# Attention and a Mish FFN on one core: the order table written anew, and ScalarE's table loads as steps of their own

## The chip, the core and the metric

The kernel runs on one core of a Trainium2 chip. A core has five engines that run side by side, each with its own queue of instructions: TensorE (PE in the profile), VectorE (DVE), ScalarE (ACT), GpSimd (POOL) and SyncE (SP, which here issues the transfers). They wait for each other through semaphores. The metric is device time in microseconds (us), lower is better.

## The reference

Attention over 4 batches x 8 heads x 768 positions x 64, with a mask by hash buckets of 6 bits, and then a feed-forward layer with the Mish function on 3072 tokens:

```python
q_bits = (einsum('bhsd,dk->bhsk', q, proj) > 0)        # k_bits in the same way
mask = q_bucket[:, :, :, None] == k_bucket[:, :, None, :]
scores = where(mask, scale * q @ k.T, -1e9)
attn = exp(scores - max(scores)); attn = attn / (sum(attn) + 1e-9)
x = (attn @ v).transpose(0, 2, 1, 3).reshape(3072, 512)
h = x @ w_in                                            # 512 x 2048
out = (h * tanh(softplus(h))) @ w_out                   # 2048 x 512
```

## The kernel before

The 3072 tokens are cut into 12 units of 256 tokens, three to a batch. A unit has 8 attention slots (4 pairs of heads x 2 halves of the unit's tokens), so there are 96 slots, n = 0 to 95, and 8 feed-forward groups of 256 hidden columns, so 96 groups, m = 0 to 95. A backbone (line 213) lists the large steps of TensorE:

- S n: scores of a slot, 8 matmuls at L878 into the banks ps_s. Behind it VectorE takes the maximum of each row (L884, "max"), derives scale and bias from it (L890, L894, L896, "scl"), and ScalarE takes the exponential twice, one head each (L909, "exp"), which frees ps_s for S n+1.
- After that the probabilities are divided and split into two halves of 16 bits: "hi" (L372, L374 or L375) and "lo" (L390, or L396 and L397), and turned by transfers (L407).
- V p: a pair of slots times the values (L992); "x_hi" and "x_lo" (L1016, L1019) write the unit's input of the feed-forward layer.
- H m: first product of a group (L1048 to L1050), then "mish" on ScalarE (L1066), "g_hi" and "g_lo" (L374 or L375, L390), then O m0 and O m1, the second product for the two halves of the tokens (L1099 to L1101).

Unit 0 is computed in 32-bit floats (S0 to S7, H0 to H7, O00 to O71, the last two at L1044 and L1095), since the weights come as 64-bit numbers that have to be made into 32-bit words first: "w_u" (L372 to L375), "w_sign" (L543, L548), "w_low" (L552, L556, L559) and "w_join" (L563) for each of 16 pieces. After a group's O the pieces are split into 16-bit halves (square L424, a small matmul L457 "st", L461, L446, "w_hi", "w_lo"), and H8, the first group of unit 1, needs the scales of all 16. Inputs of a batch are split likewise ("q_hi", "q_cp", "q_lo", "k_hi", "k_cp", "k_lo", "v_hi", "v_lo", L372 to L397).

Nothing is ordered by a scheduler when the kernel is built. Every step is recorded with its alternatives (engine and a cost in ns), and the table ORDER (L87 to L200) says in which order all 2753 steps are emitted and, by a letter b, c or d behind the number, which alternative is taken, which often means which engine. Each engine runs its own steps in that order. So ORDER decides both the order on each engine and how the work is shared out. ScalarE needs a table of functions for the exponential and another one for Mish; the compiler puts a load ahead of an activation whose table is not there. `port(...)` marks the VectorE alternatives that the search behind the table takes to share a port with GpSimd.

Of the kernel before, what the change touches and what calls it, by code (L numbers as in the profile page):

```python
# [92 lines left out]
71 205b 164 165 464 185 125c 186 188 189 190 174b 126 143b 211 212 206b 207 216b 122 187 200 201 176 167 177 178 180
202 166 191 192 197 198 308 309 372 378 193b 373 374 179 208 458 459 460 194 182d 183 199 225 203 379 128 380 184 127
204 226 248 375 227 222 223 249b 250c 251 254 230b 161 231 376c 229 228 310b 224 240 241 242 232c 233 243 244 245 311b
247 195 268 269 270 246 219c 305 271 209 265 272 196b 210 273 217 253 274b 266 255 461b 236d 237 238 262d 263 465 181
283 284 234 220 275 286 276 267 279c 285 259b 287 221 239 466 235 260 370 293c 292 294 295b 264 252 299 280 281 277
288 289 291 261 290 313c 300 301b 278 326b 462b 296 297 218b 282b 314 306 315 371 321 322 323c 324 312 327 328b 317
325 298 318 316c 432 434 329 330 344d 302 303 352 467 433 456 319 320 345 353 354 304 332b 333 435 347c 346 348 349
463 483 350 351 355 457 484 356 391 334c 335 336 337 468b 357 383b 384 385 441 485 486 392 393 338c 394 387 487 488  # L100
386 443 331 442 339 340c 341 343 503 388 396c 377b 397 381 389 398c 399 489b 444 541 395 469b 491 424 425 436 426c 400
497 527 490 402b 403b 404b 437 438 439 428 440 554 448d 405 504 505 342 406b 470 390 449 450c 452 506 401 445 492 555
580 411b 429 382 471 472 453 412 579 427b 430 493 431 407b 408b 409 410 494 495c 413b 414 358 359 507b 556 473 496
360b 474 498 475c 415 476 477c 479 451 508b 509 564 416c 480 510 454 455 499 500b 417b 557 420 361b 363 418 419 421
422c 423 542 502 516 364 517 518 501 446 565 519b 520 521c 523 362 522 566 543 478b 544 545 528 481 598 600 511 512
513b 514 567 529 530 532 365 558 546c 547 623 515 581 548 622 636 366 368 599 367 582 583 584 525 531 666 533b 534 549
550 447 524 601 602 642 585 586 482 603 536 539 369 551b 552b 553 535 537 526 559 624 625 626 587 588 627b 628b 540
589 590b 560 561 604b 629 591b 592 562 563 571c 568 538 572 574c 667 605 607 655 656 569 674 657 577b 593 594 643 644
645 646 595c 630 631 632 608 573 698 633 575 576 634c 675 647b 648 635 606b 609 610 596 597 637 614b 615 701 702 703
649 704 650 578 705c 651 570 723 616 652b 653b 706 676 677 654 707 638 639 640 713 618 641 619 708 709 715 716 724 719  # L110
720 678 717 617c 669 620 621 718 612 679 680b 658c 710 699 721b 681b 750 611 613 711c 712 700 722 659 661 714 660b 670
671b 732 683 684 746 751 860 747 748 662 663 749 672 664 754 682c 673 727 690c 691 693b 692 752b 757b 725c 726 694 728
767 798 800 733 755 729 730 665 856 731 769 695 696 697 753 807 759b 760 762 758 775 761 768 765 766 763b 764 774 770
771 808 809 810c 734 735 736 820 737c 772 773 801 790b 739 791 857 858 802 685 686 799 806 756 688 861 792 873 687 740
741 859 794 689 795 793 796 811 827 877 803c 804 805 864 821 812 813 814c 816 817 742 855 874 738c 744 862b 743 776
863 822 823b 777 778 779 878 780 781c 783 815b 818 745 875 876 825 894 909 879 880 824 847b 848 850 797 782c 895 910
784 868 869 870 871 849b 851 853 911 945 785 872 886c 887 881 882 896 826 883 786 931 828 829 884b 788 787 865 897
898b 899 830 831 842 819 888b 890b 832 833c 961 835 900 901c 902 852 889b 892b 854 932 933 789 934 912 903 668 913 914
834 964 946 962 905 843 844 845 1147 915 968 916 937b 948 891 965 966b 885 935b 938 904c 907 977 967 997 996 893 906
949 950 969 970c 971 1012 939 941 836 978 979b 951 940c 952 1011 953 908 954 955 867 837 917 846 918 980 838 840 839  # L120
942 1148 947 981 972 943 944 956 959 866 1019 973 974b 841 982 1050 957 958 975 960 919 920 921 976 922c 924 925 988c
989 990c 1102 992 1051 1052b 1046 998 999 1000 991 1047 985 993 994 995 1048c 983b 984 1001 1053 1149 1020 1021 1022
1049 1002 1003c 1004 1005c 1007 1060 1014 1015 1016b 1006 1045 1080 1008 926 927 1009 1010 923c 1064 929 928 930 1018
1017 1023b 1024 1025c 1027 1028 1032 1033 1034 1013 1031 1079 986 987 1061 1026 1029 1030 1062b 1063 1065 1094 1036
1066c 1067 1035 1037c 1038 1040 1273 1068 1039c 1041 1043 1069 1044 1055 1056 1096 1042 1095 1116 1054 1128 1057 1059
1058 1081 1070 936 1071c 1072 1074 1073c 1075 1076 1103 963 1082 1083 1117 1118 1119 1144 1085 1077 1078 1084 1086c
1087 1088 1090 1145b 1150 1146 1151 1152c 1097 1153 1339 1154 1183 1098 1099 1129 1182 1089 1155 1156b 1157 1101 1100
1104 1105 1106 1107c 1108 1091 1163 1164 1092 1131 1120b 1121 1122c 1123 1198 1132 1133b 1167 1109 1134 1124 1135 1232
1233 1168 1169b 1126 1136 1137 1093 1138c 1165c 1166 1158 1159 1110 1160 1161 1197 1140 1162 1111 1112 1113 1125 1139c
1272 1234c 1236 1237 1238b 1170 1141 1246 1247 1174 1184 1250 1235 1251 1142 1171 1185 1186 1187 1127 1130 1175 1176c  # L130
1178 1188 1114 1143 1206 1177c 1180 1179 1181 1189 1190 1207 1192 1191c 1193 1172 1194 1200 1201 1304 1202 1239 1203
1173 1205 1231 1208 1199 1240 1217 1204 1248b 1195 1209b 1210 1212 1252c 1253 1218 1219 1220 1266 1297 1211 1213 1221
# [1122 lines left out]
```

## Time and profile before

| | |
|---|---|
| median of 3 runs | 840.0 us (839.82 to 841.43) |
| profiled execution, its own time | 841.4 us |
| its span from first to last instruction | 839.6 us |
| TensorE busy | 794.9 us, 95% |
| VectorE busy | 714.6 us, 85% |
| ScalarE busy | 632.1 us, 75% |
| GpSimd busy | 93.6 us, 11% |
| granted clock of TensorE | 0.992 of full speed |

Busy times are unions of the engine's records, so a busy TensorE need not be at its peak. Times from the span's start are given as "at 172.3 us". Durations of an instruction are the means of its group.

### The profile page before, as it was taken

To read this page: it belongs to the slowest core of one execution; us is meant where nothing else is said; L and a number is where in the kernel's file an instruction comes from. 1 tells how busy PE (TensorE), PEld (TensorE's weight loads), DVE (VectorE), ACT (ScalarE), POOL (GpSimd) and SP (SyncE) were. 2 spreads that over 40 slices of the span, in tenths; PEclk is the share of its full clock that TensorE was granted. 3 is DMA by queue.
4 is the path that set the end of the run, shared out by engine and by line. 5 is a ranking of instruction groups with operands and counts; after the bars stand their busy time and mean duration, and the time that the engine had idled before them with its cause. 6 is when DMAs were issued, how large, how long until landed. Compare 5 with 4: busy or idle time off the path is not lost. (4 is left out here: it accounts for less than half of the span.)

```text
span 839.6 us, 16631 instructions
## 1 busy us (share of the span) xinstructions
PE 794.9 (95%) x6508; PEld 546.2 (65%) x6508; DVE 714.6 (85%) x1334; ACT 632.1 (75%) x972; POOL 93.6 (11%) x96
## 2 busy tenths in 40 slices
PE   4788989789999999999999999999999999999997
PEld 4656556466668578578577586577577577576664
DVE  6798999898989888989998998899999889888522
ACT  6777889987798687689878688679888688587410
POOL 5445424322230000000000000000000000000000
PEclk9899999999999999999999999999999999999999
DMA  9985878769999869899989987899997848655700
GB/s 281 197 253 178 215 179 195 120 147 186 203 181 181 165 120 158 175 171 180 185 170 175 159 176 154 142 171 196 201 157 159 168 96 160 123 95 102 157 1 26
DMA packets 400303, 135.58 MB, mean 161 GB/s; under 512 B 370528, under 2 KB 391008, under 8 KB 400224
## 3 DMA queue, kind: packets, MB, share of 16 engines
q1 hardware_dynamic: 400224, 134.52, 80.3%
q8 instruction: 51, 0.84, 0.4%
q14 instruction: 28, 0.23, 0.1%
HBM read 35.65 MB, written 6.29 MB: 50 GB/s over the span
## 5 line engine op out<-in xcount | busy, mean ns | idle before, releaser
L909 ACT ACTIVATE pb<-ps_s,svb 128x768 f32<-128x768 f32 x192 | 188.7, 986 | 58.6 <-DVE svb L896 50.6
L1048 PE MATMUL ps_acc<-X,wi 128*128 128x256 f16 x704 | 191.9, 273 | 0.8 <-ACT ffb L1066 0.8
L1050 PE MATMUL ps_acc<-X,wi 128*128 128x256 f16 x704 | 191.8, 273 | 0.0
L1049 PE MATMUL ps_acc<-X,wi 128*128 128x256 f16 x704 | 191.8, 272 | 0.0
L884 DVE TENSOR_REDUCE svb<-ps_s 128x2 f32<-128x1536 f32 x96 | 168.2, 1752 | 14.7 <-PE ps_s L878 11.1
L390 DVE SCALAR_TENSOR_TENSOR hl<-pb,svb,hl 128x768 f16<-128x768 f32 x172 | 174.5, 1022 | 6.5 <-ACT hl L374 4.0
L878 PE MATMUL ps_s<-KT,QT 128*128 128x512 f16 (+1 forms) x768 | 141.8, 328 | 6.3 <-ACT pb L909 5.3
L1099 PE MATMUL ps_o<-wo,ffb 128*128 128x512 f16 x352 | 133.4, 379 | 0.0
L1101 PE MATMUL ps_o<-wo,ffb 128*128 128x512 f16 x352 | 133.4, 379 | 0.0
L1100 PE MATMUL ps_o<-wo,ffb 128*128 128x512 f16 x352 | 133.4, 379 | 0.0
L878 PEld LDWEIGHTS <-QT 128*128 128x128 f16 x768 | 73.3, 98 | 56.6 <-issue 14.5
L374 ACT ACTIVATE hl<-pb,svb 128x768 f16<-128x768 f32 x80 | 73.4, 930 | 35.0 <-DMA PT<-hl 21.4
L992 PE MATMUL ps_t<-PT,VT 128*64 128x256 f16 x1584 | 94.6, 274 | 3.0 <-DMA PT<-hl 2.3
L1066 ACT ACTIVATE ffb<-ps_acc,smalls 128x512 f32<-128x512 f32 x88 | 59.3, 684 | 48.0 <-PE ps_acc L1050 46.9
L992 PEld LDWEIGHTS <-VT 128*64 128x64 f16 x1584 | 83.8, 110 | 17.3 <-issue 16.8
L1049 PEld LDWEIGHTS <-wi 128*128 128x128 f16 x704 | 68.8, 98 | 12.9 <-issue 1.8
L1048 PEld LDWEIGHTS <-wi 128*128 128x128 f16 x704 | 68.8, 98 | 11.6 <-issue 1.6
L1050 PEld LDWEIGHTS <-wi 128*128 128x128 f16 x704 | 68.8, 98 | 8.3 <-issue 0.2
L390 DVE SCALAR_TENSOR_TENSOR ffb<-ffb,smalls 128x512 f16<-128x512 f32 x88 | 65.2, 747 | 3.4 <-ACT ffb L374 0.9
L909 ACT ACT_TABLE_LOAD x45 | 57.7, 1283 | 12.1 <-DVE svb L896 4.7
L1101 PEld LDWEIGHTS <-ffb 128*128 128x128 f16 x352 | 34.4, 98 | 41.5
L1066 ACT ACT_TABLE_LOAD x46 | 59.0, 1283 | 0.8
(212 smaller groups left out, 991.9 us busy)
## 6 DMA issues: line engine op xcount, KB each, us to landing
out_dram<-ffb SPq DMA_DIRECT2D x24, 256.0 KB, 2.8
stg<-in_q_dram SPq DMA_DIRECT2D x10, 512.0 KB, 4.8
stg<-in_k_dram SPq DMA_DIRECT2D x12, 384.0 KB, 3.9
stg<-in_v_dram SPq DMA_DIRECT2D x12, 384.0 KB, 3.6
wo<-in_moe_w_out_dram SPq DMA_DIRECT2D x7, 512.0 KB, 4.9
stg<-in_moe_w_out_dram SPq DMA_DIRECT2D x7, 512.0 KB, 4.4
stg<-in_moe_w_in_dram SPq DMA_DIRECT2D x6, 512.0 KB, 4.5
wi<-in_moe_w_in_dram SPq DMA_DIRECT2D x6, 512.0 KB, 4.5
```

The source lines that it names most:

```text
L390: return [("DVE", 215 + 1.035 * n, port(lambda: nc.vector.scalar_tensor_tensor(out=dst, in0=src, scalar=sc, in1=hi, op0=ALU.mult, op1=ALU. ...
L878: nc.tensor.matmul(sc[:, hh * S + c0 * P:hh * S + c1 * P], QTb[:, u % 2, sl, qi], KTb[:, j, sl, hh * NCH + c0:hh * NCH + c1].rearrange("p ...
L884: op("max", [("DVE", 1790, lambda: nc.vector.tensor_reduce(out=sv[:, 0], in_=sc.rearrange("p (h e) -> p h e", h=2), axis=AX.X, op=ALU.max, ...
L909: EXP[n, hh] = op("exp", [("ACT", 1075, lambda hh=hh, t=t: nc.scalar.activation(pb[:, t], sc[:, hh * S:(hh + 1) * S], AF.Exp, bias=sv[:, 2 ...
L992: nc.tensor.matmul(pv[hh * D:(hh + 1) * D, 0:256], vt[:, w, hh * NCH + c], pt[:, hh, a * NCH + c].rearrange("p s t -> p (s t)"), start=(x ...
L1048: nc.tensor.matmul(o, wh, X[:, 0, c], start=(c == 0), stop=False)
L1049: nc.tensor.matmul(o, wh, X[:, 1, c], start=False, stop=False)
L1050: nc.tensor.matmul(o, wl, X[:, 0, c], start=False, stop=(c == NCC - 1))
L1066: op("mish", [("ACT", 690, lambda: nc.scalar.activation(ffb[:, t], PS[psn], AF.Mish, scale=h))], [psn] + ([(hsn, g, g + 1)] if u else []), ...
L1099: nc.tensor.matmul(PS[f"o{s}"], gh, hi[:, e], start=first, stop=False)
L1100: nc.tensor.matmul(PS[f"o{s}"], gh, lo[:, e], start=False, stop=False)
L1101: nc.tensor.matmul(PS[f"o{s}"], gl, hi[:, e], start=False, stop=last)
```

## The change

Two new steps are recorded. Ahead of the two exponentials of each slot stands "pre_e", ahead of each Mish "pre_m". Each has two alternatives: a load of the table as an instruction of its own, or nothing. They have no predecessors and no readers, so they can stand anywhere in the order. The numbers of all later steps move on, and the table is a new one throughout, 2945 steps; of it the diff shows the first line.

```diff
 ORDER = """
-37 88 14 22 7 0 3 1 2 23 24 25 63 73 38c 6 8 9 13 10 15 152 5 4 40 41 18 19 42 74 11b 12 20 21 26c 53b 75 76 77b 43 28
...
+1 155 0 3 14 22 2 23 24 25 38c 4 40 7 6 8 9 5 10 41 11 12 13 37 18 19 63 73 20 21 26c 42 43 74 44 75 490b 76 39 28b 15
...
     def att_exp(n):
         sv, x = svb[:, n % NSV], f"sv{n % NSV}"
         sc, scn = scores(n)
+        op("pre_e", [("ACT", 1290, lambda: nc.scalar.preload_act_table(AF.Exp)), ("ACT", 0, lambda: None)])
         for hh in range(2):
...
         h = hs[:, g:g + 1] if u else 1.0
+        op("pre_m", [("ACT", 1290, lambda: nc.scalar.preload_act_table(AF.Mish)), ("ACT", 0, lambda: None)])
         op("mish", [("ACT", 690, lambda: nc.scalar.activation(ffb[:, t], PS[psn], AF.Mish, scale=h))],
```

The steps themselves and their data are the same. In the new table 43 pre_e and 22 pre_m are loads, the others nothing; where a table is then still missing the compiler loads it as before, 15 times ahead of an exponential and 32 times ahead of a Mish. With the first load of the program that makes 113 loads where there were 92. The sharing of the work among the engines changes too. On GpSimd, w_sign goes from 8 to 10, v_hi from 2 to 4, w_low from 3 to 4; hi goes from 8 to 5, lo from 4 to 2, v_lo from 2 to none, sums from 6 to 2, k_cp from 4 to 1, g_hi from 4 to none. The lines of the new program lie 9 (up to pre_e), 10 and 11 (behind pre_m) further down.

ScalarE around the Mish of H5 in unit 0 (L909 exp, L1066 mish; in the new program L919 and L1077, the explicit loads L916 and L1076). Before:

```order
L1066 ACT_TABLE_LOAD
L1066 ACTIVATE ffb<-ps_acc_820 128x512
L374 ACTIVATE tok_64<-X,smalls 128x16x64
L424 ACTIVATE wi,smalls<-wi 128x1024
L909 ACT_TABLE_LOAD
L909 ACTIVATE pb,svb<-ps_s,svb 128x768
L1016 ACTIVATE X<-ps_t,smalls 128x256
```

Now:

```order
L1076 ACT_TABLE_LOAD
L1026 ACTIVATE X<-ps_t,smalls 128x256 x2
L1077 ACTIVATE ffb<-ps_acc_824 128x512
L916 ACT_TABLE_LOAD
L433 ACTIVATE wo,smalls<-wo 128x1024
L433 ACTIVATE wi,smalls<-wi 128x1024
L919 ACTIVATE pb,svb<-ps_s,svb 128x768 x2
```

The load of Mish's table now stands two activations ahead of the Mish, and that of the exponential two squares ahead of it.

GpSimd, the end of its queue (L372 hi and g_hi, L396 and L397 the two instructions of a lo, L381 w_home). Before:

```order
L381 TENSOR_SCALAR wo<-stg 128x1024
L372 TENSOR_SCALAR hl<-pb,svb 128x768
L372 TENSOR_SCALAR ffb<-ffb,smalls 128x512
L372 TENSOR_SCALAR hl<-pb,svb 128x768
L396 TENSOR_SCALAR pb<-pb,svb 128x768
L397 TENSOR_TENSOR hl<-pb,hl 128x768
L372 TENSOR_SCALAR ffb<-ffb,smalls 128x512
L890 TENSOR_SCALAR svb<-svb,smalls 128x2
L896 TENSOR_TENSOR svb<-svb 128x2
L372 TENSOR_SCALAR hl<-pb,svb 128x768
```

Now, up to the last instruction:

```order
L406 TENSOR_TENSOR hl<-pb,hl 128x768
L455 TENSOR_SCALAR smalls<-smalls 128x2
L455 TENSOR_SCALAR smalls<-hw 128x1
L381 TENSOR_SCALAR tok_64<-stg,smalls 128x12x64
L390 TENSOR_SCALAR tok_65<-tok_64 128x12x64
L405 TENSOR_SCALAR pb<-pb,svb 128x768
L406 TENSOR_TENSOR hl<-pb,hl 128x768
```

The new queue of GpSimd ends with steps of S16 and S17 and of the inputs of batch 1. What it did later, of slots 18 to 24, is with VectorE and ScalarE now.

VectorE between the max of S29 and that of S30 (L375 hi, L390 lo and g_lo; now L384 and L399). Before:

```order
L390 SCALAR_TENSOR_TENSOR hl<-pb,svb,hl 128x768
L375 TENSOR_SCALAR ffb<-ffb,smalls 128x512
L390 SCALAR_TENSOR_TENSOR ffb<-ffb,smalls 128x512 x2
L642 TENSOR_SCALAR smalls<-ho,smalls 128x8
L446 TENSOR_SCALAR smalls<-smalls 128x8
L1019 SCALAR_TENSOR_TENSOR X<-ps_t,smalls,X 128x256
L390 SCALAR_TENSOR_TENSOR ffb<-ffb,smalls 128x512
L931 RECIPROCAL svb<-svb 128x2
L375 TENSOR_SCALAR hl<-pb,svb 128x768
L390 SCALAR_TENSOR_TENSOR hl<-pb,svb,hl 128x768
```

Now:

```order
L384 TENSOR_SCALAR hl<-pb,svb 128x768
L399 SCALAR_TENSOR_TENSOR hl<-pb,svb,hl 128x768 x2
L784 TENSOR_SCALAR smalls<-smalls 128x4
L455 TENSOR_SCALAR smalls<-smalls 128x4
L399 SCALAR_TENSOR_TENSOR ffb<-ffb,smalls 128x512
L935 TENSOR_SCALAR svb<-svb 128x1 x2
L941 RECIPROCAL svb<-svb 128x2
L384 TENSOR_SCALAR hl<-pb,svb 128x768
L859 TENSOR_SCALAR smalls<-smalls 128x4
L399 SCALAR_TENSOR_TENSOR hl<-pb,svb,hl 128x768
```

Between the two stand one hi and one lo of the attention more, and one g_hi and two g_lo fewer.

## Rows read from the trace of the kernel before

**Rows 1.** The page: busy times, and TensorE in 40 slices of the span.

```profile
PE 794.9 (95%) x6508; PEld 546.2 (65%) x6508; DVE 714.6 (85%) x1334; ACT 632.1 (75%) x972; POOL 93.6 (11%) x96
...
PE   4788989789999999999999999999999999999997
```

**Rows 2.** Busy time by stage: stretch, length, engines (with instructions), clock, DMA share, GB/s.

```profile
0.00:40.00 40.00, 25.10 (x242) 20.79 (x244) 27.27 (x80) 28.54 (x45) 19.76 (x25) 0.91 0.94 241
40.00:106.00 66.00, 58.59 (x360) 38.90 (x359) 61.89 (x98) 52.51 (x75) 29.34 (x26) 0.97 0.76 217
106.00:171.00 65.00, 54.22 (x357) 34.87 (x355) 60.31 (x98) 58.81 (x87) 22.44 (x24) 0.97 0.77 160
171.00:272.00 101.00, 97.58 (x869) 70.06 (x869) 92.00 (x194) 84.61 (x135) 22.09 (x22) 1.00 0.98 182
272.00:800.00 528.00, 524.05 (x4452) 358.79 (x4451) 463.08 (x851) 403.49 (x627) 0.00 (x0) 1.00 0.83 156
```

**Rows 3.** TensorE's largest wait from 180 us on: total us, times, longest.

```profile
PE ps_s L878 <- ACT pb L909: 2.6, 5, 0.7
```

**Rows 4.** TensorE's timeline: S18, a small matmul, the first of H9, the last small one.

```profile
169.26 1.90 PE L878 MATMUL ps_s<-KT,QT 128*128 128x512 f16 x8 [0.26 <-ACT pb L909]
...
172.25 0.16 PE L457 MATMUL ps_t<-smalls,ones 128*128 128x1 bf16 x1 [0.76 <-ACT wo L424]
...
172.30 0.27 PE L1048 MATMUL ps_acc<-X,wi 128*128 128x256 f16 x1
...
177.14 0.16 PE L457 MATMUL ps_t<-smalls,ones 128*128 128x1 bf16 x1 [1.89 <-ACT wo L424]
```

**Rows 5.** VectorE's timeline: the max of S18 and the max of S30.

```profile
175.50 1.75 DVE L884 TENSOR_REDUCE svb<-ps_s 128x2 f32<-128x1536 f32 x1
...
272.85 1.75 DVE L884 TENSOR_REDUCE svb<-ps_s 128x2 f32<-128x1536 f32 x1
```

**Rows 6.** VectorE's groups from 0 to 171 us: count | busy us, mean ns | idle before.

```profile
L543 DVE TENSOR_SCALAR wo<-stg 128x1024 int16<-128x1024 int16 x3 | 2.3, 755 | 0.1
L375 DVE TENSOR_SCALAR VT<-wo,smalls 128x768 f16<-128x768 f32 x1 | 1.6, 1556 | 0.0
L390 DVE SCALAR_TENSOR_TENSOR VT<-wo,smalls,VT 128x768 f16<-128x768 f32 x1 | 1.0, 1010 | 0.0
L390 DVE SCALAR_TENSOR_TENSOR wo<-wo,smalls 128x1024 f16<-128x1024 f32 x5 | 6.4, 1276 | 0.0
L943 DVE COPY X<-ps_g 128x256 f32<-128x256 f32 x3 | 1.3, 417 | 0.0
L890 DVE TENSOR_SCALAR svb<-svb,smalls 128x2 f32<-128x2 f32 x14 | 7.0, 500 | 0.4
```

**Rows 7.** VectorE's groups from 171 to 272 us.

```profile
L390 DVE SCALAR_TENSOR_TENSOR hl<-pb,svb,hl 128x768 f16<-128x768 f32 x22 | 22.1, 1014 | 0.4
L375 DVE TENSOR_SCALAR hl<-pb,svb 128x768 f16<-128x768 f32 x6 | 3.7, 614 | 0.1
L390 DVE SCALAR_TENSOR_TENSOR tok<-stg,smalls,tok 128x768 f16<-128x768 f32 x3 | 3.6, 1187 | 0.1
```

**Rows 8.** VectorE's groups from 272 us on, where GpSimd does nothing.

```profile
L890 DVE TENSOR_SCALAR svb<-svb,smalls 128x2 f32<-128x2 f32 x60 | 13.7, 228 | 1.8
```

**Rows 9.** GpSimd's w_sign, whole span.

```profile
L548 POOL TENSOR_SCALAR wo<-wo 128x1024 bf16<-128x1024 int16 x2 | 4.5, 2273 | 2.9 <-ACT wo L556 2.2 <-DVE wo L375 0.6
L548 POOL TENSOR_SCALAR wi<-stg 128x1024 bf16<-128x1024 int16 x1 | 1.4, 1350 | 0.0
```

**Rows 10.** ScalarE's table loads as groups, and one on its timeline.

```profile
L909 ACT ACT_TABLE_LOAD x45 | 57.7, 1283 | 12.1 <-DVE svb L896 4.7
...
179.66 0.19 ACT L909 ACTIVATION_READ_ACCUMULATOR pb<-ps_s,svb 128x1 f32 x1
179.87 1.28 ACT L1066 ACT_TABLE_LOAD   x1
181.17 1.27 ACT L1066 ACTIVATE ffb<-ps_acc,smalls 128x512 f32<-128x512 f32 x2
```

More of the change, by code (lines that the diff above doesn't have):

```diff
@@ L93 @@
[L93 to L132, printed above, removed]
@@ new lines @@
+737 645 744 747 754 646 647 550b 278b 749 727 696 706 743 738 685 782 745 739c 695 686 688 777 746 750b 755b 707 787
+687c 740 742b 783b 689 690 763 751 784 897 638 708 709b 779 1193 637 697 639 711 712 698 756 780c 691 692 781 701 700
+718c 719 720c 722 723 721 757 758 759 800 832 785b 834 892 724 725 788 790b 791 762 786 761 792 793 794c 809 795 710
+764 796 798 799 802 803 804 842 797 843 844 801 845c 765 806 766 767 768c 770 807 1306 894 1116b 808 824 825 855 771
+713 714 895b 835 833 841 891 826 836 805 1104b 715 716 837 717 896 936 839 828 829 935 840 789 846 847c 899 863 848
@@ new lines @@
+905 1016b 1024 1007 1046 1121b 1026 748 1518 1017 870c 1045 1061 1062 982c 1027c 993 873 1029 984 925c 926 874 875
+1343b 876 877 995 996 997 998 983 1028 1070 999c 985 1099 986 987 1031 1018 1032c 1033 1097 1001 1002 1067 1019 1020
+961 962 963 964 965c 967 966c 990 1000c 1207 1003 1004 1022 1023 1037 1098 1100 1208 1101b 1038 1039 968 1103 1105
+1047 1115 1048 1049 1051 1040c 1041 1052 1043 882 1034 1035 1042 1071 1072 1102 1053b 1054 1055c 1108 1057 1346 1073
+1044 1064 1056 1065 1066 1069 1059 1068 1137 1063 969 970 1106c 1107 1074b 971 1075 1117 1118b 972 1120 1122 1076c
@@ new lines @@
+1078 1083 1084 1058 753b 760 1085 1088 1119 1077c 1036 1087 1089c 1080 1082 1136 1152 1060 1090 1091c 1123b 1093 973
+1153 1175 1079 1092 1109 1095 1110 1111 1674b 1125 1126 1114 1154 1113 1124 979 1161 1127 1162 621b 1223b 1128c 1081
+1129 1130 1094 1131 1187 1138 1139 1140 1096 1176 1177 1178 1132 1133 1142 1134 1135 1204 1210 1143 1144b 1215 1145
+1784 1209 1212 1205 1213c 1214 1248 1163 1146 1148 1164 1149 1155 1217 1188b 1247 1252b 1218b 1165 1166b 1219 1263
+1264 1189 1147 1158 1156 1157 1160 1167c 1168 1169 1150 1151 1226 1159 1379 1228 1179b 1180 1181c 1182c 1183 1190 1191
@@ new lines @@
+1352 1293c 1295 1353b 1311 1312 1313 1325b 1326 1354c 1281 1294 1442b 1297 1355 1316 1315 1330b 1393 1318b 1327 1328
+1329 1438 1439 1296 1331 1333 1340 1341 1342 1779b 1283 1332 1334 1372 1405 1406b 1463b 1705b 1344 1298 1336 1345
+1362c 1363 1394 1395 1396 1414 1364 1366 1373 1356 1380 1357 1358 1359 1374 1360 1375 1441 1381 1216 1443 1444c 1382
+1445 1446 1480 1454 1377 1481 1335 1378 1408 1440 1365c 1337 1368 1383 1582 1397 1398 1367 1399 1448 1449b 1384c 1386
+1401 1369 1409 1450 1400 1403 1457 1459 1460b 1467 1468 1410 1470c 1413 1471 1986b 1512 1387 1388 1469 1361 1385c 1402
@@ new lines @@
+1389 1461 1390 1391 1412 1430b 1431 1572 1404 1416 1432c 1434 1417 1489 1451 1452 1453 1574 1433 1436 1112b 1462 1464
+1455 1465c 1418 1392 1419 1456 1435 1437 1592 1466 1594 1420 1421c 1423 1422c 1424 1488 1577 1579 1472 1473 1474c
+1475c 1485 1476 1482 1483 1484 1477 1486 1513 1573b 1478 1479 1522 1525c 1526 1487 1504c 1543 1597 1515 1505 1506c
+1523 1524 1521 1508 1509 1516 1425 1426 1580b 1571 1407 1427 1428 1429 1211b 1575b 1490 1491 1507 1517 1520 1519 1576
+1227b 1492 1493 1494 1510 1514 1535 1536 1599 1495c 1527 1511 1497 1542 1637 1615 1616 1581 1632 1528 1529 1602 1498
@@ new lines @@
+1537 1538 1540 1531 1541 1532 1530c 1533 1534 1563c 1564 1586 1631 1565 1496 1595c 1596 1654 1567 1568 1587 1600b 1603
+1566 1544 1545 1569 1570 1588 1591 1590 1499 1633 1500 1601 1546 1547 1585 1668 1669 1558 1559 1604 1560 1561 1607
+1608 1610c 1609 1548 1617 1618 1619b 1655 1288 1656 1657 1621 1611 1613 1622 1501 1612 1584 1640 1710 1623 1502 1605b
+1624 1625c 1627 1549c 1685 1688 1690 1691c 1686 1692 1626 1458b 1634 1503 1635 1693 1725 1232b 1583 1726 1614 1695
+1696b 1697 1887 1742 1589 1636b 1639 1551 1550c 1638 1628 1447 1704 1629 1741 1706 1707b 1606 1660 1661 1662c 1663
@@ new lines @@
+1671 1664 1730 1708 1552 1641 1630 1672 1673 1553 1554 1555 1750 1743 1676 1675 1677c 1642 1912 1778 1780 1665 1698
+1709 1562 1795 1556 1557 1643 1644 1645c 1781b 1647 1648 1678 1680 1666 1667 1649 1711 1783 1699 1782 1593b 1700 1702
+1679c 1681 1682 1703 1717c 1683 1684 1646c 1727 1650 1712c 1713 1762 1620b 1796 1714 1785 1797 1651 1539 1718 1652
+1653 1719c 1721 1720 1728 1729 1732 1786c 1787 1723 1731 1733b 1734 1735c 1737 1751 1752 1744 1745 1746 1841 1715 1753
+1788 1816 1798b 1658b 1722 1736 1739 1749 1694b 1748 1724 1799 1777 1687 1800 1763 2023b 1754 1755 1756c 1738 1832
@@ new lines @@
+1985 1874 1376b 1598 1980 1876 1864 1982 1866 1877 1878c 1880 1873 1900 1901 1902b 1914b 1792b 1915 2026 2028 1879c
+1882 2027 1904 1905 1983c 1952 1919 1920 1921c 1881 2029 1997 1999 1968b 1578b 1987 1923 1883 1916 1917 1924 1922c
+1929 1930 1931 1998b 2059 1821b 1886 1891b 1943 1945 1988c 2095 1838 1869 2122b 1925 1926 1989 2002 1984 1934 1933
+1946 1918 1935c 1936 1938 1937c 1947 1948 1950 1939 1940 1951 1941 1942 1964 2018 2000c 2001 1953 1954 1955 1956c 1957
+1903 1958 1965 1966 1967 1960 1979 1959 1961 1962 1969 2050 2019 2051 1970 1971c 1991 2052 1972 1973c 1975 1976 1992
@@ new lines @@
+2545 2624 2632 2528 2591 2554 2556b 2557 2580 2660 2544 2529 2558c 2560 2581 2582 2559 2530 2593 2546 2594c 2549 2427
+2561 2531 2670 2585 2584 2599c 2562 2600 2601c 2662 2665 2667 2768 2609 2596 2597 2603 2610 2611 2614 2563 2682 2604
+2602c 2605 2648b 2606 2613 2615c 2595 2527c 2616 2617 2663c 2664 2533 2532 2534 2626 2627 2628 2619 2618c 2620 2684
+2621 2668c 2669 2677 2679 2644 2698 2633 2630 2680c 2851b 2631 2645 2636b 2637 2638c 2640 2646 2647 2650 2649 2651c
+2639c 2659 2699 2566 2685b 2598 2715 2678b 2634 2622 2681 2846b 2642 2652 2653 2641 2654c 2657 2643 2761b 2658 2655
@@ new lines @@
+2741b 2927b 2852 2817 2720 2785 2786c 2795 2796 2788 2781 2789 2818 2894b 2798 2917b 2853c 2854 2799 2800b 2801 2802c
+2787 2790 2811 2803 2810 2844 2860 2812 2858b 2813 2815 2804 2816 2830 2806 2553 2821 2822 2791 2823c 2825 2829 2782
+2868 2870 2805 2824 2819 2807 2831 2832 2826 2869 2871 2859 2873 2827 2828 2835 2834 2836 2837 2872 2839 2838c 2840
+2841 2842 2783 2861b 2820 2843 2862 2863c 2864 2865 2866 2867 2880 2592b 2881 2882 2874 2875 2876 2899b 2877 2883 2885
+2886c 2887 2888 2904 2878b 2903 2890 2891c 2879 2892 2906 2905 2893 2895 2898 2900 2896c 2897 2908 2907 2901c 2902
@@ L200 @@
+2909 2703b 2910 2911 2916 2913 2914c 2915 2932 2814b 2918 2919c 2920 2931 2933 2777 2934 2921 2923 2924c 2925 2926
+2936 2928 2929c 2930 2922b 2935 2937 2938b 2772b 2939b 2940 2941 2943b 2942b 2944
 """
```

139 lines of the change are left out of this document (68 added, 71 removed).

## The prediction

> **What bounds the kernel now.** First the page: TensorE is busy 794.9 us of 839.6, and its slices show a ragged start of about nine slices and then 9 throughout [rows 1]. So two stages have to be told apart, and the view of busy time by stage does that [rows 2]. From 272 to 800 us TensorE is busy 524.05 of 528 us at full clock; from 171 to 272 us it is busy 97.58 of 101. From 180 us on its largest wait is 2.6 us in five pieces [rows 3]. Whatever the other engines do there, TensorE can give back some 4 us and no more; a new order can only lose there.
>
> The first 171 us are different. TensorE idles 14.9 us up to 40 us, 7.4 from there to 106 and 10.8 from there to 171 [rows 2]. The engine that is full is VectorE: 61.89 of 66 us, then 60.31 of 65. It idles 8.8 us in those 131 us. That it is behind and not merely busy is seen at S18: the scores start at 169.26 and take 1.90 us, and their max begins at 175.50, 4.3 us after they were there [rows 4, 5]. ScalarE idles 13.5 and 6.2 us in the two stages. The first group of unit 1 (H9) starts at 172.30, and from 177 us on TensorE stays full [rows 2, 4]. So the time is about 175 us of a stage that VectorE paces, then a stream of TensorE work that the change leaves as it is, then the same stores.
>
> **The stage that VectorE paces.** I counted VectorE's steps in either order up to the max of S18. They are 252 in both, but not the same ones. Fewer in the new order: two w_sign and two w_low, passes over 1024 columns at 0.755 us [rows 6], 3.0 us; one v_hi, 1.556 us where it stood [rows 6], 1.6; two rvc at 0.417 [rows 6], 0.8; one lo at 1.014 and one hi at 0.614 [rows 7], 1.6. That is 7.0 us off. More: two v_lo at 1.010 [rows 6], 2.0; one w_lo at 1.276 [rows 6], 1.3. Six small steps come too (three copies, two sums, one pw) while one q_lo goes. For the small ones I have bounds alone: nothing, or the 0.417 of rvc each, 2.5 in all [rows 6]; I take the middle, 1.2, since half of them are copies and half are tiny. One ob comes and one w_hi goes, passes of about the same length. Sum: -7.0 + 2.0 + 1.3 + 1.2 = -2.5 us, with ends at -3.7 and -1.2. If VectorE's idle time there stays what it is, all that hangs on the max of S18 comes 2.5 us earlier, H9 and H8 with it.
>
> **The next stage, 171 to 272 us.** In the new order GpSimd has nothing left to do here, and its 22.09 us [rows 2] go to VectorE and ScalarE. Between the max of S18 and that of S30 VectorE gets 8 hi, 3 lo and 2 v_hi more and one k_hi less (g_hi, g_lo and small ones come and go). That is 9 x 0.614 + 3 x 1.014 = 8.6 us [rows 7]. Three things make it less. A record begins about 0.1 us before the one ahead has ended, so 12 steps in a full queue cost 1.2 less. The input's lo took 1.187 beside GpSimd, where the same size elsewhere takes 1.014 [rows 7], three of them, 0.5. Other steps lose their GpSimd neighbour as well, which I bound by nothing and 2 us and take at 1. So +5.9 us. VectorE idles 9.0 of 101 us there [rows 2], and the new order has one O more ahead of S30, 1.3 us of TensorE. That leaves 9.0 + 1.3 - 5.9 = 4.4 us of idle time, 4%, if TensorE is not to wait. In the stages before it VectorE idled 6% and 7%, so it is tight. I take no wait: the steps that came in are hi and lo, which feed a V two slots later, and TensorE has H and O to do meanwhile. Were that cover gone, up to 4.6 us would come back (second rival).
>
> **The table loads.** A load takes 1.283 us and the activation starts 0.02 us behind it [rows 10]. 21 loads more are 26.9 us of ScalarE. ScalarE is idle 839.6 - 632.1 = 207.5 us [rows 1], and behind 175 us TensorE does not wait for it beyond rows 3, so they cost nothing I can see. What an explicit load may bring is that it runs while the exponential's scale is still awaited: 12.1 us of idle time stand ahead of the 45 loads for the exponential [rows 10], 0.27 each. Up to S18 there are ten loads in both orders, and four of the ten are explicit now. With VectorE as the pace I count nothing for it, and the bound is 4 x 1.283 = 5.1 us if each stood on the path.
>
> **Sum.** The profiled execution took 841.4 us for a span of 839.6; the median of three runs is 840.0. -2.5 us makes 838.9 of the one and 837.5 of the other. I give the median: **837.5 us**. A measurement of this kernel tells about 0.2% from no change, so faster means under 838.3 and slower over 841.7.
>
> **The rivals.**
>
> *The explicit loads do stand on the path.* If the early stage is set by the round of S, max, scl, exp, and not by VectorE's sum, four explicit loads take up to 5.1 us off on top: 832.4. For it: the first 40 us, where VectorE idles 12.7 [rows 2], are such rounds. Against it: no load falls into them but the program's first, the max of S18 waits for VectorE, and in the order two of the four loads merely change places with squares that ScalarE has to do anyway.
>
> *VectorE becomes the pace from 171 to 272 us.* One mechanism, at S19 to S30: VectorE cannot give up its 9.0 us of idle time, since hi waits for ScalarE's sums and lo for hi. Then the max of S30 comes 5.9 us later against S18, TensorE has 1.3 us of that covered, and it waits 4.6. With the early gain that is 840.0 - 2.5 + 4.6 = 842.1, without it 844.6. It decides once VectorE needs more than the 4.4 us of idle time left. For it: the 6% and 7% above. Against it: TensorE's queue is full of other work, and VectorE's steps are behind by microseconds, so that they find their inputs ready.
>
> *GpSimd holds VectorE up for longer.* The scl of two columns takes 0.500 us up to 171 us and 0.228 from 272 on, where GpSimd does nothing [rows 6, 8]; a v_hi took 1.556 there and a pass of the same size 0.614 [rows 6, 7]. The new order puts two w_sign more on GpSimd, of 1.35 to 2.27 us [rows 9]. If each holds one VectorE step for its length, 2.7 to 4.5 us are lost and the 2.5 are eaten: 840.2 to 842.0, and I take 840.5. For it speak those rows; against it, that two v_lo and one w_lo leave GpSimd up to S18, two instructions each and as long. The Trainium skill, "SBUF — State Buffer", section "SBUF: two separate sides", says that VectorE and GpSimd share a pair of ports as an exclusive lock, and that whichever starts first has it for its whole instruction. By that rule the two w_sign would each block a VectorE step that needs the pair, which is this rival; the trace agrees as far as the 0.500 against 0.228 goes, and how many steps meet such an instruction no row shows.
>
> **How the numbers follow.** Forecast (835 to 839.5): 0.40. Loads on the path: 0.13. VectorE late behind 171 us: 0.25. Gain eaten by GpSimd or not there: 0.22. Faster: three quarters of the first, the second and a little of the last, 0.30 + 0.13 + 0.03 = 0.46. Within 0.2%: the rest of the first and most of the last, 0.10 + 0.19 = 0.29. Slower: 0.25, the third. The range for 8 in 10 runs from 831.5, just under the loads' case, to 844.5, the third case without the early gain. The likeliest case alone would be 835 to 839.5.
>
> **What would show it.** Right: H9 or H8 of unit 1 starts 2 to 3 us earlier than 172.30 and 177.14; VectorE's idle time from 40 to 171 us is still about 9 us; from 180 us on TensorE's waits sum to under 6 us. The loads' rival: the max of S12 and S18 comes 5 us or more earlier than VectorE's sum allows. The second rival: waits of TensorE for the exponential between 180 and 275 us that sum to 4 us or more, with VectorE at 95% there. The third: scl and the other short VectorE steps longer than 0.500 us before 171 us. The forecast is wrong in its root if the early stage comes out several microseconds off in either direction with VectorE's work as counted: then its idle time sets that stage, not its sum.

## The result, and the profile after

The changed kernel takes 850.0 us (median of 4 runs, 848.5 to 851.5) where the kernel before takes 840.7 beside it: ratio 1.0105, interval 1.0075 to 1.0136. The forecast was 837.5 us with a range from 831.5 to 844.5; the kernel became 1% slower, by about 9 us. The profiled execution has a span of 847.8 us and a granted clock of 0.984 (before: 839.6 and 0.992).

The page of the kernel after, as [rows 1]: engine, busy us, share, instructions; then TensorE in 40 slices.

```profile
PE 797.1 (94%) x6508; PEld 546.6 (64%) x6508; DVE 717.6 (85%) x1371; ACT 658.3 (78%) x996; POOL 68.8 (8%) x72
...
PE   4879987869999999999999999999999999999998
```

The ragged start lasts into the ninth slice as before, and is hollower in the seventh and ninth (7 and 6 where there were 9 and 8). Busy time by stage, columns as in [rows 2]:

```profile
0.00:40.00 40.00, 25.59 (x250) 19.60 (x252) 28.00 (x82) 28.14 (x46) 20.47 (x30) 0.96 0.94 247
40.00:106.00 66.00, 56.97 (x350) 37.95 (x346) 57.28 (x95) 49.33 (x72) 29.87 (x23) 0.95 0.69 199
106.00:171.00 65.00, 54.10 (x329) 35.51 (x330) 55.37 (x104) 52.21 (x76) 16.62 (x18) 0.92 0.76 162
171.00:272.00 101.00, 92.97 (x785) 64.27 (x784) 94.75 (x191) 89.19 (x140) 1.89 (x2) 0.97 0.88 172
272.00:800.00 528.00, 523.70 (x4497) 360.09 (x4496) 469.39 (x880) 432.22 (x655) 0.00 (x0) 1.00 0.85 158
```

From 272 us on next to nothing changed: TensorE idles 4.3 of 528 us, against 4.0, and its largest wait from 180 us on is smaller than in [rows 3]:

```profile
PE ps_s L887 <- ACT pb L919: 1.5, 3, 0.9
```

The loss is earlier. The max of S18 begins 8.3 us later than in [rows 5], and the max of S30 still 11.3 later:

```profile
183.83 1.75 DVE L893 TENSOR_REDUCE svb<-ps_s 128x2 f32<-128x1536 f32 x1
...
284.14 1.76 DVE L893 TENSOR_REDUCE svb<-ps_s 128x2 f32<-128x1536 f32 x1 [0.41 <-PE ps_s L887]
```

From the max of S18 to the end of the span it is 664.1 us before and 664.0 after. The 3 us that S30 is late on top are a place in the order, given back later: between the two maxima TensorE is busy 97.97 us after and 95.07 before, so it does more work ahead of S30 now, and idles 2.3 us in both. So the whole loss lies ahead of S18. Busy time up to the max of S18, before and after:

```profile
0.00:175.50 175.50, 141.27 (x984) 97.16 (x985) 153.79 (x286) 144.25 (x212) 72.69 (x76) 0.96 0.81 201
```

```profile
0.00:183.83 183.83, 142.40 (x967) 96.51 (x968) 152.56 (x305) 141.73 (x214) 68.84 (x72) 0.93 0.76 191
```

VectorE (the third figure behind the length) has 1.2 us **less** to do up to that point, and 31.3 us of idle time instead of 21.7. What TensorE waits for, whole span (total, times, longest):

```profile
PE ps_acc L1054 <- ACT ffb L1077: 5.2, 1, 5.2
PE ps_t L466 <- ACT PT L433: 5.0, 1, 5.0
PE ps_t L1009 <- DVE X L1022: 4.5, 1, 4.5
PE ps_o L1106 <- ACT ffb L1077: 4.4, 2, 4.0
PE ps_t L466 <- DVE hsum L725: 3.3, 1, 3.3
```

The second is the program's start and stands in the kernel before too. The others are four single places, of which three were taken up (the fourth, the hsum, is the sum of the hash bits at 179 us).

**Place 1, V1 at 54.8 us.** V1 waits for x_32 of V0 (unit 0's form of x_hi and x_lo, one step of VectorE that reads what V left in ps_t). Its inputs were there at 44.2 us. On VectorE's timeline x_32 is the last row: ahead of it stand the max of S5, its scl (0.97 us beside GpSimd), a w_join, a w_sign. In the kernel before V1 does not wait (second fence).

```profile
48.45 1.75 DVE L893 TENSOR_REDUCE svb<-ps_s 128x2 f32<-128x1536 f32 x1
50.24 0.97 DVE L899 TENSOR_SCALAR svb<-svb,smalls 128x2 f32<-128x2 f32 x1
...
51.32 1.22 DVE L572 SCALAR_TENSOR_TENSOR wi<-wo,wi 128x1024 int32<-128x1024 int32 x1
...
52.58 1.37 DVE L552 TENSOR_SCALAR wo<-stg 128x1024 int16<-128x1024 int16 x1
...
54.30 0.41 DVE L1022 SCALAR_TENSOR_TENSOR X<-ps_t,X 128x256 f32<-128x256 f32 x1
```

```profile
51.85 2.81 PE L999 MATMUL ps_t<-PT,wi 128*64 128x256 f32 x24
```

**Place 2, O30 at 108.7 us.** ScalarE's timeline: the mish of H3 (last row) has had its product since 102.9 us, but a square stands ahead of it that waits 3.74 us for a w_lo of VectorE.

```profile
102.00 1.16 ACT L383 ACTIVATE stg<-stg 128x1024 f32<-128x1024 f32 x1 [0.19 <-POOL wi L557]
106.89 1.06 ACT L433 ACTIVATE wi<-wi 128x1024 bf16<-128x1024 f32 x1 [3.74 <-DVE wi L399]
...
107.94 0.58 ACT L1077 ACTIVATE ffb<-ps_acc 128x512 f32<-128x512 f32 x1
```

VectorE is late there, with GpSimd at work beside it: w_sign, w_lo and lo take 2.75, 3.25 and 1.87 us, beside a w_low, a w_sign and a w_u on GpSimd (second fence).

```profile
96.78 2.75 DVE L552 TENSOR_SCALAR wi<-wo 128x1024 int16<-128x1024 int16 x1
99.43 3.25 DVE L399 SCALAR_TENSOR_TENSOR wo<-wo,smalls,stg 128x1024 f16<-128x1024 f32 x1
102.60 1.87 DVE L399 SCALAR_TENSOR_TENSOR hl<-pb,svb,hl 128x768 f16<-128x768 f32 x1
```

```profile
96.03 2.87 POOL L561 TENSOR_SCALAR wi<-wi 128x1024 int16<-128x1024 uint16 x1 [5.22 <-DMA wi<-in_moe_w_in_dram]
98.99 2.88 POOL L557 TENSOR_SCALAR wi<-wi 128x1024 bf16<-128x1024 int16 x1
101.95 1.72 POOL L381 TENSOR_SCALAR wi<-wi 128x1024 f32<-128x1024 f32 x1
```

**Place 3, H7 at 140.4 us.** This is the piece of ScalarE's queue shown with the change: the load of Mish's table, then two x_hi, then the mish. The second x_hi waits 4.82 us for an x_lo, and the mish, whose product has been there since 133.9 us (H5 runs from 130.14 for 3.72 us) and its table since 134.05, stands behind it.

```profile
132.77 1.28 ACT L1076 ACT_TABLE_LOAD   x1
134.07 0.47 ACT L1026 ACTIVATE X<-ps_t,smalls 128x256 f16<-128x256 f32 x1
139.36 0.47 ACT L1026 ACTIVATE X<-ps_t,smalls 128x256 f16<-128x256 f32 x1 [4.82 <-DVE X L1029]
139.73 0.59 ACT L1077 ACTIVATE ffb<-ps_acc 128x512 f32<-128x512 f32 x1
```

**Such a wait is paid twice.** The windows of V1's wait, of V1, and of the first 2.9 us of H7 behind the third wait (TensorE's busy time is the first figure behind the length, VectorE's the third, granted clock third from the end):

```profile
50.30:54.76 4.46, 0.01 (x2) 0.01 (x1) 4.37 (x8) 3.26 (x6) 3.52 (x4) 0.85 0.55 186
54.76:60.15 5.39, 5.39 (x25) 2.74 (x26) 0.00 (x0) 0.22 (x1) 0.00 (x0) 0.50 0.93 141
...
140.37:143.30 2.93, 2.93 (x7) 2.39 (x8) 1.88 (x3) 2.92 (x4) 0.00 (x0) 0.50 0.73 138
```

TensorE had idled 4.46 us, and the 24 matmuls of V1 then run at a granted clock of 0.50, the lower of its two levels (1.2 GHz): 5.39 us, where the experiment on this place (e5) shows 2.81 for the same 24 at 1.00. VectorE, which next needs V1, does nothing at all in those 5.39 us. That is more than half of the 9.6 us that it idles more.

### The profile page after: what moved, and what is told of

Read it like the earlier page. It is cut to its first block, busy times and chain, and to the rows that moved or that the text cites. A ratio compares the mean times of both kernels' runs of the same rounds, so it can differ in the third digit from the quotient of the medians.

```text
span 847.8 us, 16654 instructions
## 1 busy us (share of the span) xinstructions
PE 797.1 (94%) x6508; PEld 546.6 (64%) x6508; DVE 717.6 (85%) x1371; ACT 658.3 (78%) x996; POOL 68.8 (8%) x72
## 5 line engine op out<-in xcount | busy, mean ns | idle before, releaser
L919 ACT ACTIVATE pb<-ps_s,svb 128x768 f32<-128x768 f32 x192 | 188.4, 985 | 47.5 <-DVE svb L905 34.2
L399 DVE SCALAR_TENSOR_TENSOR hl<-pb,svb,hl 128x768 f16<-128x768 f32 x174 | 177.2, 1026 | 6.6 <-ACT hl L383 4.2
L1077 ACT ACTIVATE ffb<-ps_acc,smalls 128x512 f32<-128x512 f32 x88 | 59.3, 684 | 41.8 <-PE ps_acc L1060 33.8
L383 ACT ACTIVATE hl<-pb,svb 128x768 f16<-128x768 f32 x77 | 70.8, 929 | 19.5 <-DMA PT<-hl 7.7
L1058 PEld LDWEIGHTS <-wi 128*128 128x128 f16 x704 | 68.8, 98 | 11.3 <-issue 1.2
L399 DVE SCALAR_TENSOR_TENSOR ffb<-ffb,smalls 128x512 f16<-128x512 f32 x88 | 65.6, 747 | 2.9 <-ACT ffb L383 1.0
L1112 PEld LDWEIGHTS <-ffb 128*128 128x128 f16 x352 | 34.4, 98 | 41.7 <-DVE ffb L399 0.3
L384 DVE TENSOR_SCALAR hl<-pb,svb 128x768 f16<-128x768 f32 x94 | 57.7, 617 | 1.9 <-DVE svb L941 0.3
L1111 PEld LDWEIGHTS <-ffb 128*128 128x128 f16 x352 | 34.4, 98 | 36.5
```

The lines of the kernel that those rows point to most:

```text
L383: ACT=lambda: nc.scalar.activation(dst, src, AF.Copy, scale=sc),
L399: return [("DVE", 215 + 1.035 * n, port(lambda: nc.vector.scalar_tensor_tensor(out=dst, in0=src, scalar=sc, in1=hi, op0=ALU.mult, op1=ALU. ...
L1058: nc.tensor.matmul(o, wh, X[:, 0, c], start=(c == 0), stop=False)
L1111: nc.tensor.matmul(PS[f"o{s}"], gh, lo[:, e], start=False, stop=False)
L1112: nc.tensor.matmul(PS[f"o{s}"], gl, hi[:, e], start=False, stop=last)
```

## The experiments

Theory A: steps that stand in the wrong place of an engine's queue in the first 180 us make TensorE and VectorE wait; the sum of the work has little to do with it. B: the table loads cost the time. C: the work taken from GpSimd behind 171 us does. D: the early stage is paced by the sum of VectorE's work, as the prediction had it. In the cuts of ORDER below each line is one step, and steps that are left out stand as "...". All runs are in one table. The two middle columns are from the profiled execution, whose first 30 us scatter by up to 4 us at the same order (the max of S1 came at 30.0, 26.2, 30.2 and 30.1 us in e8 to e11), so the ratio decides. Counted from the max of S1 instead, the max of S18 comes after 147.0 us before, 155.7 in the kernel after, 149.1 in e5, 156.1 in e6, 155.6 in e7, 146.8 in e8, 146.6 in e9 and 143.7 in e10.

| run | max of S18 | from there to the end | ratio to before, interval |
|---|---|---|---|
| before | 175.5 | 664.1 | 1 |
| after | 183.8 | 664.0 | 1.0105 (1.0075 to 1.0136) |
| e1_no_loads | 185.6 | 682.9 | 1.0357 (1.0326 to 1.0388) |
| e2_loads_alone | 175.3 | 670.5 | 1.0080 (1.0055 to 1.0105) |
| e12_loads_in_place | 174.2 | 663.6 | 0.9993 (0.9974 to 1.0013) |
| e3_start_before | 175.5 | 667.0 | 1.0041 (1.0019 to 1.0063) |
| e4_start_after | 183.7 | 664.7 | 1.0101 (1.0070 to 1.0131) |
| e5_x32_early | 178.5 | 664.2 | 1.0030 (1.0018 to 1.0042) |
| e6_mish_first_no_port | 185.5 | 663.6 | 1.0092 (1.0076 to 1.0108) |
| e7_mish_before_xhi | 183.5 | 663.2 | 1.0067 (1.0050 to 1.0085) |
| e8_three_mended | 176.8 | 663.4 | 0.9996 (0.9980 to 1.0012) |
| e9_st_later | 172.7 | 665.8 | 0.9998 (0.9982 to 1.0014) |
| e10_xlo_exp_first | 174.0 | 663.7 | 0.9950 (0.9931 to 0.9969) |
| e11_half_early | 172.3 | 665.9 | 0.9954 (0.9929 to 0.9978) |

**The new order without its loads.** Each pre_e and pre_m of the table gets the letter b, which means nothing, as these two do:

```diff
-591
+591b
...
-405
+405b
```

> The new kernel with its new order, but none of the 65 explicit table loads: the compiler puts a load where a table is missing, as in the kernel before. If the loss of 10 us comes of the order of the first 180 us (theory A), the time stays at 848 to 853 us, and S19 still starts at 188 to 191 us. If it comes of the explicit loads (theory B: 21 loads more at 1.283 us, and loads that stand ahead of other work), most of the loss goes: 840 to 844 us. If it comes of GpSimd's work having been moved to VectorE behind 171 us (theory C), nothing changes: about 850 us.

Measured: 872.0 us, 22 us slower than the kernel after. All three theories missed. The loss ahead of S18 stays (A), but 19 us come behind it. ScalarE's loads of this run:

```profile
L1078 ACT ACT_TABLE_LOAD x52 | 66.7, 1283 | 1.2 <-DVE ffb L400 0.3
L920 ACT ACT_TABLE_LOAD x51 | 65.4, 1283 | 45.9 <-DVE svb L906 30.2 <-DVE svb L904 10.6 <-DVE smalls L471 4.7
```

and those of the kernel after:

```profile
L916 ACT ACT_TABLE_LOAD x43 | 55.2, 1283 | 0.7
L1077 ACT ACT_TABLE_LOAD x32 | 41.1, 1283 | 0.8 <-DVE ffb L399 0.3
L1076 ACT ACT_TABLE_LOAD x22 | 28.2, 1283 | 0.4
L919 ACT ACT_TABLE_LOAD x15 | 19.2, 1283 | 7.6 <-DVE svb L903 4.2 <-DVE svb L905 3.2
```

The compiler's load stands behind the wait of the activation that it serves: 45.9 us of idle time in front of 51 of them, for the bias and scale from VectorE. An explicit one waits for nothing: 0.7 us in front of 43. In this run S waits 14.0 us in 17 places for the exponential from 230 to 800 us, in the kernel after 1.5 in 3. The new order needs the early loads: without them S18 to the end takes 682.9 us. That these waits make up all of the 19 us isn't shown. B is out as a cause of the loss.

**Loads alone, on the order of before.** Two forms of the same 91 loads. In e2 each stands right behind the last activation of the other table, in e12 right in front of the activation that needs it; for one Mish (753 is the load, 754 the mish, 668 an exponential, 736 to 744 steps of other engines):

```diff
 668
+753
 645
...
 744
 754
```

```diff
 668
 645
...
 744
+753
 754
```

> The order and the sharing of the kernel before, with explicit loads alone: each of the 91 changes of table gets its load as an instruction of its own, as early as it can stand, right behind the last activation of the other table. Theory A: the loads cost and bring next to nothing, 838.5 to 841.5 us. Theory B: loads as instructions of their own cost time by themselves, 845 us or more. If instead loads on the path were worth something, as the first rival of the prediction had it, up to 5 us come off: 835 us.

> The order and the sharing of the kernel before, each of its 91 changes of table as an instruction of its own, but where it stood: directly in front of the activation that needs it. Nothing is moved past anything; the load only does not wait any more for what the activation waits for (12.1 us of idle time stood in front of the 45 loads for the exponential). Theory A (a load costs only what it pushes back, and is worth only its own wait): 838.5 to 841.5 us, ratio 0.996 to 1.001, without the 6 us that early loads cost. Theory B (loads as instructions of their own cost time by themselves): 845 us or more, as with the early loads.

Measured: 847.5 us for the early ones, where theory A had at most 841.5; nothing is lost up to S18 (175.3 us). 840.7 for those in place, as A had it, no difference from the kernel before. The loads in place do lose the wait (12.1 us of idle time in [rows 10]):

```profile
L916 ACT ACT_TABLE_LOAD x45 | 57.7, 1283 | 0.8
```

but TensorE's largest wait from 180 us on is as in [rows 3]:

```profile
PE ps_s L887 <- ACT pb L919: 2.5, 5, 0.7
```

What ScalarE wins there TensorE had no use for. The two runs differ in the place of the loads alone, so the place cost 6 us: from 175 us on TensorE's waits sum to 11.6 us in e2, and to 6.3 in the kernel before. I take it that a load moved ahead of other activations pushes each of them back by its 1.283 us; no run follows that one by one. B names the size of e2 rightly, and the place not at all: the kernel after loses everything ahead of S18 and nothing behind.

**Which stage.** Up to S19 (696) the steps of the one table, then the rest in the order of the other (here a line holds several steps). Against the table of the kernel after, e3 changes the start and e4 what is behind S19, with no explicit load there:

```diff
-1 155 0 3 14 22 2 23 24 25 38c 4 40 7 ...
+37 88 14 22 7 0 3 1 2 23 24 25 63 73 ...
...
 696
```

```diff
 696
-706 743 738 685 782 745 739c 695 ...
+743 706 745 746 638 707 708b 685c ...
...
```

> Steps in the order of the kernel before, with its sharing, up to the scores S19; from there the order, the sharing and the explicit loads of the new kernel. Theory A: S19 starts at about 180 us as before and the rest takes as long as in either kernel: 839.5 to 842 us. Theory C (the later stage is slower for VectorE's added work): 847 to 851 us. Theory B (65 explicit loads, of which only those behind S19 are in it, nearly all): 847 to 850 us.

> The counterpart: the new order, sharing and its few explicit loads up to the scores S19, then the order and the sharing of the kernel before, with no explicit load. Theory A: S19 starts at 188 to 190 us and the whole takes 848 to 851 us. Theory B or C: most of the loss is behind S19 and goes with it, 840 to 843 us.

Measured: 844.2 us, between what A and what C had expected, and 850.2, as A had it. The start of the new order costs 9 us with either rest behind it; C is out. That the new rest behind the old start costs 3 us shows at the max of S19 (188.0 us instead of 184.7); in the kernel after the same rest costs nothing, so I take it for the price of the seam, which no run took apart.

**The three places, one by one and together.** Each run is the kernel after with the steps of one place moved, first x_32 of V0 (217; 205 is the max of S4, 317 an st, 200 a copy for another V, 261 is V1):

```diff
 205
+217
 317
...
 200b
-217
 261
```

> The new kernel with one step moved on VectorE: x_32 of V0 (ready at 44.2 us) stands behind the max of S4 instead of behind the max and scl of S5, a w_join, a w_sign and two bits. Theory A (idle time put in by the order of single steps): V1 starts at about 50.3 instead of 54.8 us, the max of S6 comes at about 59 instead of 63.1 us, and of these 4 us between 1 and 4 are left at the max of S18 (183.8 us now) and at the end: 846 to 849 us. Theory D (the stage is paced by the sum of VectorE's work, as the prediction had it): the max of S6 comes earlier, that of S18 does not, 850 us.

Measured: 844.5 us, better than the 846 that A had as its best: more than half of the loss is gone with one step of 0.41 us. D, which had 850, is out as the whole account. V1 starts at 51.93 and takes 2.81 us:

```profile
51.93 2.81 PE L1009 MATMUL ps_t<-PT,wi 128*64 128x256 f32 x24
```

The second place (459 is H3, 461 its mish, 360 a lo, 403 and 404 max and scl of S11, 414 and 415 the w_low and w_sign, whose new letters put them on VectorE):

```diff
 360
+403
+404b
...
 459
+461
...
-403
-404b
...
-461
...
-414
-415b
+414c
+415
```

> The new kernel with the stall at 104 to 109 us taken apart. On ScalarE the mish of H3 stands in front of a w_u and a square that waits for VectorE; on VectorE the max and scl of S11 stand in front of a w_join and a w_lo; and a w_low and a w_sign go from GpSimd to VectorE and to a place 13 us later, so that GpSimd is silent while VectorE works on w_sign, w_lo and lo (2.75, 3.25 and 1.87 us in the new kernel, where forms of that size take 0.75, 1.27 and 1.01 without GpSimd). Theory A: those three take about 3 us instead of 7.9, the max of S11 comes at about 100 instead of 106.7 us, O30 does not wait 4.0 us, and 2 to 6 us are left at the end: 844 to 848 us. Theory D: VectorE has 1.5 us more to do, so 850 to 852 us.

Measured: 849.2 us, no gain that stands out of the noise, where A had 844 to 848. The place itself is mended: without GpSimd beside them the three steps take 0.74, 1.26 and 1.01 us, and the max of S11 comes at 100.8.

```profile
98.06 0.74 DVE L552 TENSOR_SCALAR wi<-wo 128x1024 int16<-128x1024 int16 x1
98.70 1.26 DVE L399 SCALAR_TENSOR_TENSOR wo<-wo,smalls,stg 128x1024 f16<-128x1024 f32 x1
99.89 1.01 DVE L399 SCALAR_TENSOR_TENSOR hl<-pb,svb,hl 128x768 f16<-128x768 f32 x1
100.81 1.75 DVE L893 TENSOR_REDUCE svb<-ps_s 128x2 f32<-128x1536 f32 x1
```

But on TensorE a small st now waits 3.43 us for a square, and the 16 matmuls of H4 behind it take 6.62 (0.71 and 3.70 in the kernel after):

```profile
116.78 0.16 PE L466 MATMUL ps_t<-smalls,ones 128*128 128x1 bf16 x1 [3.43 <-ACT wo L433]
...
116.83 6.62 PE L1054 MATMUL ps_acc<-X,wi 128*128 128x256 f32 x16
```

The 6 us won at S11 are gone at S13. The third place (579 is the mish of H5, 588 a load of its table):

```diff
 588
+579
 580
...
-579
 405
```

> The new kernel with one step moved on ScalarE: the mish of H5 stands right behind the load of its table, in front of the two x_hi, of which the second waits 4.8 us for VectorE. Theory A: the mish comes at about 134 instead of 139.7 us, H7 does not wait 5.2 us for it, and 2 to 5 us are left at the end: 845 to 848 us. Theory D: 850 us.

Measured: 847.8 us; 3 us less by the ratios, whose intervals overlap, and 1.1 by the spans, so that a gain isn't shown for this edit alone. H7 no longer waits, and the st behind it does, 4.84 us, with H6 at a mean granted clock of 0.61 behind that (16 matmuls, 6.02 us; H7's take 3.62):

```profile
135.41 3.62 PE L1054 MATMUL ps_acc<-X,wi 128*128 128x256 f32 x16
143.86 0.16 PE L466 MATMUL ps_t<-smalls,ones 128*128 128x1 bf16 x1 [4.84 <-ACT wi L433]
...
143.92 6.02 PE L1054 MATMUL ps_acc<-X,wi 128*128 128x256 f32 x16
```

> The three edits of the other runs of this call together, in the new kernel. Theory A: the gains add up in the most part, the max of S18 comes at 175 to 178 us instead of 183.8, and the time is 840 to 844 us, about that of the kernel before. Theory D: 849 to 852 us.

The three edits at once. Measured: 842.1 us, ratio 0.9996. Five steps moved and two put on another engine, out of 2945, give the whole loss back, as A had it. By the ratios the single runs give 6, 1 and 3 us, together 9; the intervals don't tell that from their sum. Over e5 the other two places bring 3 us, with intervals that don't touch. How much of these 3 comes of the order, and how much of the two steps that GpSimd lost, no run tells apart.

**Further along the chain.** On top of that on TensorE three large steps in front of the st that wait (510 behind H4, 574, and 563 behind H6, 587; S18, 663, in front of the st 730), with the small steps that read these st:

```diff
-510
 417
 574
+510
...
-563
...
 587
+563
...
+663
 730
...
-663
```

> The three mended edits together, and on TensorE three of the small matmuls st moved to the other side of a large step: the st that waits 2.9 us for a square behind H4, the one that waits 4.8 us behind H6, and S18 in front of the st behind the hsum. Theory A (each step of TensorE that stands in front of work that is ready costs its wait): S18 starts at about 168 to 171 us instead of 173.5, and the time is 836 to 840 us, the first version under the kernel before (ratio 0.994 to 0.998). Theory D or a wait that only takes another name, as it was with the mish of H5 alone: 841 to 843 us, ratio 0.999 to 1.001.

Measured: ratio 0.9998, nothing, where A had 0.994 to 0.998. The waits only took other places: TensorE's from 40 to 190 us sum to 22.1 us, against 21.7 in e8 (27.4 in the kernel after, 21.1 in the kernel before). Then, around S14, the x_lo of V5 (537) with two x_hi (536, 463) in front of the max, and the exponentials (520 is the last) in front of two squares (529, 562). Last the half (614, the step of VectorE that reads an st and so frees its bank) for V6 in front of a k_lo (633) and a scl (583):

```diff
 579
+536
+537
+463
...
-536
-537
-463
...
-529
...
-562
...
 520
+529
+562
```

```diff
 582
-583b
-633
 613
 614
+583b
...
+633
```

> The kernel with the st moved, and around S14 the x_lo of V5 in front of the max on VectorE, so that the x_hi of V4 does not wait 4.4 us for it on ScalarE, and on ScalarE the exponentials of S14 in front of two squares. Theory A: the exponentials of S14 come at about 135 instead of 138.9 us, S15 3 us earlier, and 1 to 3 us of it are left at the end: 834 to 839 us. Theory D: no change against the run with the st moved.

> The kernel of the run above, and on VectorE the half that frees the bank for V6 in front of a k_lo and a scl. Theory A: V6 does not wait 2.0 us, up to 1.5 us less than the run above. Theory D: no change.

Measured: 838.0 and 838.3 us, ratios 0.9950 and 0.9954: faster than the kernel before by 0.5% and than the kernel after by 1.5%. The last edit brings nothing more. Whether the edits of e10 would do it without those of e9 was not tried. The two middle stages of e10:

```profile
40.00:106.00 66.00, 60.95 (x382) 40.61 (x381) 61.79 (x111) 57.05 (x82) 24.52 (x23) 1.00 0.80 225
106.00:171.00 65.00, 52.53 (x352) 34.74 (x351) 58.45 (x114) 55.87 (x84) 20.51 (x20) 0.93 0.78 165
```

VectorE idles 10.8 us there, 18.4 in the kernel after and 8.8 in [rows 2].

## Why the prediction was wrong

The loss came where the prediction had expected a gain, up to S18; none of its rivals put a loss of this size there.

- **TensorE bounds the kernel behind 177 us and has nothing to give: right.** 664.1 and 664.0 us from the max of S18 to the end.
- **VectorE's work up to S18 falls by 2.5 us, ends -3.7 and -1.2: at the small end.** 153.79 to 152.56, -1.2 us. The count had left out one scl that comes to VectorE, 0.500 us by [rows 6].
- **"If VectorE's idle time there stays what it is": the step that failed.** It rose from 21.7 to 31.3 us. I read a stage at 94% and 93% of VectorE's time as one that VectorE paces, and so took its idle time for a constant. In these runs it is set by what stands in front of what on the engines' queues. Theory D expected no change from moving one step of 0.41 us; e5 moved it and won 6 us, with VectorE's work nearly the same (151.8 us up to the max of S18) and its idle time down to 26.7. The prediction had compared which steps stand ahead of S18, and not, for a single V, H or O, which step of another engine it waits for and what stands in front of that one. Its last sentence had named this as the way to be wrong in its root: the early stage off by several microseconds with VectorE's work as counted.
- **The place was in the text.** The order of ScalarE around the mish of H5 was shown with the change, and it put two x_hi between a load and its mish. I read it as a statement on the load. What the x_hi wait for was not asked, and 4.82 us of wait stood there. (Mending this place alone won nothing sure, e7.)
- **The price of a wait was left out.** Nothing in the sum held the granted clock. Up to S18 it fell from 0.96 to 0.93, and behind a wait of 4.5 us V1 took 5.39 us instead of 2.81.
- **Loads cost and bring nothing: right for the old order, with the loads in place, and wrong for the new one.** In place they are worth nothing (0.9993). In the new order they are worth 22 us. Up to S18, where my bound was 5.1, it is 2 (185.6 against 183.8); the other 19 lie behind S18, where I had counted nothing, since in the rows of the old order TensorE does not wait for a load. What loads are worth depends on the order that they stand in.
- **Rival, VectorE as the pace from 171 to 272 us: did not happen.** VectorE's work between the max of S18 and that of S30 rose by 4.3 us (5.9 forecast), from 88.53 to 92.82, and TensorE idled 2.3 us there in both kernels.
- **Rival, GpSimd holds VectorE up longer: not in sum.** Up to 180 us VectorE's instructions take 16.4 us longer before and 17.1 after than their forms take undisturbed (each length less the tenth percentile of its operation and shape over both kernels, added up; with the tiles told apart as well it is 13.5 and 12.9). Either way the two are less than 1 us apart, and the two-column scl takes 0.486 us up to 171 us, against 0.500 before. e6 took 4.9 us away from three of these instructions, and by itself won nothing sure.

What stays open is the seam of e3, what e6 and e7 each add to e5, and the share of the fourth place (the hsum at 179 us), which e9 touched without a gain.

## What to carry to other kernels

With queues that run in order, ask for each large matmul which single instruction releases it, and what stands in front of that one on its own queue; an engine that is busy 93% of a stage need not pace it, since its remaining idle time can grow. In two of the three places here the mended wait turned up one step later, so follow the chain behind a mended place. A table load as an instruction of its own is worth the wait that it no longer shares, and can cost what it pushes back; both have to be counted in the order that uses it.
